# Padding four small tiles so that the buffers behind them in SBUF begin at multiples of 256 bytes

## The chip, the cores and the metric

One Trainium2 chip, of which the kernel uses one core. A core has a tensor engine (PE; its weight loads stand apart as PEld), a vector engine (DVE), a scalar engine (ACT), GpSimd (POOL), a sync engine (SP) that here does little but issue DMAs, and 16 DMA engines that move data between HBM and SBUF, the on-chip memory of 128 partitions. The metric is the time of one execution on the device in microseconds (us); lower is better. "Start" of an SBUF buffer means its byte offset within each partition.

## The reference

Two stages, both in float32. The first is block-sparse attention over 4 batches, 8 heads, 768 positions and a head size of 64: blocks of 32 positions; a query block sees its neighbours, the first and the last block, and three sampled blocks; the first and last query blocks see everything.

```python
scores = scale * np.matmul(q, k.transpose(0, 1, 3, 2))
scores = np.where(mask, scores, -1000000000.0)
scores = scores - np.max(scores, axis=-1, keepdims=True)
attn = np.exp(scores)
attn = attn / (np.sum(attn, axis=-1, keepdims=True) + 1e-09)
return np.matmul(attn, v).astype(np.float32)
```

The second is a feed-forward layer on the 3072 x 512 result, with a rational function between its two products:

```python
h = x @ w_in
P = a[0] + a[1] * h + a[2] * h2 + a[3] * h3
Q = 1.0 + np.abs(b[0]) * np.abs(h) + np.abs(b[1]) * h2
g = P / (Q + 1e-06)
return (g @ w_out).astype(np.float32)
```

The weights come as float64; the kernel turns them into narrower types itself.

## The kernel before

The kernel writes down some thousands of small operations (class `Op`), each with an engine, a price, what it follows and which buffers it takes, and `issue` lays them out on the engines by those prices before the kernel runs. So the order on each engine is fixed when the program is built, and no byte address enters it: changing where a tile lies doesn't change the order.

Keys: a tile of 128 positions of k is loaded (L580, 256-byte runs, one per head and position) into `tt`, `ab`, `sq` for batch 0 and into `ld` for the later ones, transposed on PE (L555) and copied out (L150), for batch 0 into `kall` and later into `kt`, from where L598 stores it to a scratch tensor `ks` in HBM. For the later batches each pair of query blocks gathers its key blocks from `ks` (L777 to L785) into one of three buffers: two halves of `kall`, which is free by then, or `xkg`, a third buffer of the same size. All three are used for the same work in turn.

Queries: L681 loads 128 positions of q into `ldq` in 256-byte runs; PE transposes them (L555).

Values: L913 to L923 gather value blocks from v straight into one of four buffers `vg`, in 512-byte runs. A single block goes to 16 of the 128 partitions, three neighbours to 48, a whole row of blocks (L913) to all 128. The values' product is L944, the scores are L821, the transposes of the probabilities L898. v is also loaded once to find its scale (L646, into `tt`, `ab`, `sq`, `ld`).

Weights: the raw float64 w_in is loaded (L437) into the memory of `wo_l` and `wo_b`; the raw w_out (L432) into `wl`. DVE, ACT and POOL decode both (L446 to L453, and L150, L154, which are one helper for many copies); the working words are `wi` for w_in and `dw` for w_out.

The feed-forward layer runs in units of 256 tokens by 256 hidden columns: products into `ph` (L1040 to L1042), the rational function on ACT and DVE (L1047 to L1085), and products into `acc` (L1097 to L1103). L162 is a filler matmul that the planner puts into PE's gaps in the first part.

SBUF tiles are placed one behind the other, pool by pool, in the order in which a pool first meets them. Three places make small ones: `scales` takes a tile of 4 floats under the names `scw` and `sc1` (three buffers each), `wscale` holds 8 floats, and `most`, in `weights`, takes `sums`, of 8 floats (two buffers). The large buffers behind them begin where these end.

Of the kernel before, what the change touches and what calls it, by code (L numbers as in the profile page):

```python
# [11 lines left out]
F32 = mybir.dt.float32  # L12
# [12 lines left out]
def kernel(  # L25
# [30 lines left out]
    P = 128  # L56
# [10 lines left out]
    NU = NF // 2  # L67
# [8 lines left out]
    const = ctx.enter_context(tc.tile_pool(name="const", bufs=1))  # L76
# [3 lines left out]
    p4 = ctx.enter_context(tc.tile_pool(name="p4", bufs=4))  # L80
    early_cm = tc.tile_pool(name="early", bufs=2)
    early = early_cm.__enter__()
# [50 lines left out]
    def row(eng, steps, after, prio, takes=(), uses=()):  # L133

        o, after = None, list(after)
        for n, (price, run) in enumerate(steps):
            o = Op(eng, price, run, [o] if n else after, prio, takes=() if n else takes, uses=list(uses) + (list(takes) if n else []))
        return o
# [3 lines left out]
    def among(key, home, **prices):  # L142

        d = {{"ve": VE, "sc": SC, "po": PO}[n]: p for n, p in prices.items()}
        return {home: d[home], **(d if key in ALT else {})}

    def times(eng, out, in_, by):

        if eng is nc.scalar:
            nc.scalar.activation(out=out, in_=in_, func=AF.Copy, scale=by)  # L150
        elif eng is nc.vector and isinstance(by, float) and by == 1.0:
            nc.vector.tensor_copy(out=out, in_=in_)
        else:
            eng.tensor_scalar(out=out, in0=in_, scalar1=by, scalar2=0.0, op0=ALU.mult, op1=ALU.add)  # L154
# [181 lines left out]
    def scales(get, name, after, prio, slot=(), finish=None, keep=None):  # L336


        res, d = [], {}
        s_ps = Slot(r_sp)  # L340

        def most():
            d["pt"] = banks[s_ps.buf]
            nc.tensor.transpose(d["pt"][:, :P], get().broadcast_to([P, P]), ident)

        def largest():
            m = p4.tile([P, 4], F32, name=name, bufs=3)
            res.append(m)
            nc.vector.tensor_reduce(out=m[:, 0:1], in_=d["pt"][:, :P], axis=AX.X, op=ALU.max)

        def floor():
            nc.vector.tensor_scalar(out=res[0][:, 0:1], in0=res[0][:, 0:1], scalar1=2.0 ** -100, scalar2=None, op0=ALU.max)

        def exponent():
            mi = res[0].bitcast(I32)
            nc.vector.tensor_scalar(out=mi[:, 1:2], in0=mi[:, 0:1], scalar1=0x7F800000, scalar2=None, op0=ALU.bitwise_and)

        def power():
            m, mi = res[0], res[0].bitcast(I32)
            nc.vector.tensor_scalar(out=mi[:, 2:3], in0=mi[:, 1:2], scalar1=-1.0, scalar2=float((2 * 127 + 14) << 23), op0=ALU.mult, op1=ALU.add)  # L360
            nc.vector.tensor_scalar(out=mi[:, 3:4], in0=mi[:, 1:2], scalar1=float(14 << 23), scalar2=None, op0=ALU.subtract)
            res[:] = [m[:, 2:3], m[:, 3:4]]
            if keep:
                keep(*res)

        def final():
            finish(*res)

        a = Op(TE, 109, most, after, prio, takes=[s_ps])
        a = Op(VE, 260, largest, [a], prio, takes=slot, uses=[s_ps])  # L370
        return row(VE, [(69, floor), (69, exponent), (138, power)] + ([(138, final)] if finish else []), [a], prio, uses=slot), res

    scrap = const.tile([P, 512], F16, name="scrap")

    def head(c, g):

        return 2 * c + g
# [3 lines left out]
    def bound(src, mx):  # L381

        nc.scalar.activation(out=scrap[:, :src.free_size()], in_=src, func=AF.Abs, accum_out=mx)
# [6 lines left out]
    wo_h = const.tile([P, NF, DM], F32R, name="wo_h")  # L390
    wo_l = const.tile([P, NF, DM], BF16, name="wo_l")
    wo_b = const.tile([P, NF, DM], BF16, name="wo_b")
    wscale = const.tile([P, NU], F32, name="wscale")
    in_ready, out_ready, scale_ready, decoded, freed, whole = {}, {}, {}, [], {}, {}


# [5 lines left out]
    def weights():  # L402
# [10 lines left out]
        sums, before, begun = {}, [None, None], {}  # L413

        def raw(u, x):
            x0 = (x // 2 if u == 0 else 2 + x // 2) * NCC
            home = [wo_l, wo_b][x % 2][:, x0:x0 + NCC]
            return home.rearrange("p a n -> p (a n)").bitcast(I32)

        def homes(x):  # L420
            x //= NCC
            return [freed[0 if x < 2 else NG - 1, 2 * (x % 2) + y] for y in range(2)]

        def one(prio, kind, u, x, before):
            d = {}
            s_wl = Slot(r_wl) if kind else None
            s_w = Slot(r_dw) if kind else None

            def load():
                d["ld"] = early.tile([P, 2 * WC], I32, name="wl", bufs=2) if kind else raw(u, x)  # L430
                if kind:
                    nc.sync.dma_start(out=d["ld"], in_=wo64[x * P:(x + 1) * P])  # L432
                    return
                r0 = head(x, 0) * D
                if u == 0 and x == 0:
                    nc.gpsimd.tensor_copy(out=d["ld"][:, 0:1].bitcast(F32), in_=kall[:, 12, 0, 0:1])
                (nc.sync if u > 1 else nc.gpsimd).dma_start(out=d["ld"], in_=wi64[r0:r0 + P, u * 2 * WC:(u + 1) * 2 * WC])  # L437

            def convert(eng):
                d["w"] = early.tile([P, WC], I32, name="dw", bufs=3) if kind else wi[:, x, u].rearrange("p a n -> p (a n)").bitcast(I32)  # L440
                d["words"] = d["ld"].rearrange("p (n w) -> p n w", w=2)
                times(eng, d["w"].bitcast(F32), d["words"][:, :, 1].bitcast(F32), 2.0 ** -112)

            def pack1():
                w = d["w"]
                nc.vector.tensor_scalar(out=w, in0=w, scalar1=3, scalar2=None, op0=ALU.logical_shift_left)  # L446

            def pack2():
                nc.vector.scalar_tensor_tensor(out=d["w"], in0=d["words"][:, :, 0], scalar=29, in1=d["w"], op0=ALU.logical_shift_right, op1=ALU.bitwise_or)  # L449

            def pack3():
                to = d["w"] if kind else d["words"][:, :, 0]
                nc.vector.scalar_tensor_tensor(out=to, in0=d["words"][:, :, 1], scalar=-2 ** 31, in1=d["w"], op0=ALU.bitwise_and, op1=ALU.bitwise_or)  # L453
                if not kind:
                    whole[u, x] = to.bitcast(F32)

            def most():
                if u not in sums:
                    sums[u] = early.tile([P, 8], F32, name="sums")
                bound(whole[u, x], sums[u][:, x:x + 1])  # L460

            def out_high(eng):
                times(eng, wo_h[:, x], d["w"].bitcast(F32), 1.0)

            def out_short(eng):
                times(eng, wo_b[:, x], d["w"].bitcast(F32), 1.0)

            def out_low(eng):
                eng.tensor_tensor(out=wo_l[:, x], in0=d["w"].bitcast(F32), in1=wo_h[:, x].bitcast(F32), op=ALU.subtract)

            wl = [s_wl] if kind else []
            if kind or u > 1:
                o0 = Op(SY, [(475, 524288)], load, [o_setup] if kind else [freed[u - 1, x]], prio - 2, takes=wl, behind=before[kind])
            else:
                o0 = Op(PO, [(700, 524288)], load, [k_evac[0][3]] if u == 0 else [begun[0, x]], -17.0 + 1.2 * x if u else -84, behind=before[kind])
            before[kind] = o0
            w = [s_w] if kind else []
            o = Op(among("c", SC, sc=520, po=588, ve=335), 0, convert, [o0], prio, takes=w, uses=wl)
            if not kind:
                begun[u, x] = o  # L480
            o = Op(VE, 335, pack1, [o], prio, uses=w)
            o = Op(VE, 602, pack2, [o], prio, uses=wl + w)
            o = Op(VE, 602, pack3, [o], prio, uses=wl + w)
            if kind:
                o1 = Op(among("o", SC, sc=520, po=588, ve=335), 0, out_high, [o], prio, uses=w)
                o2 = Op(among("p", PO, po=1225, ve=602), 0, out_low, [o1] + homes(x), prio, uses=w)
                o3 = Op(among("q", SC, sc=520, po=588, ve=335), 0, out_short, [o] + homes(x), prio, uses=w)
                out_ready[x] = [o2, o3]
                decoded.append(o3)
                decoded.append(o2)  # L490
                return o2
            return Op(SC, 613, most, [o], prio)

        group = []
# [755 lines left out]
```

## Time and profile before

| what | value |
|---|---|
| runs | 833.17 us median of 3 (833.16 to 833.39) |
| profiled execution | 832.03 us, of which the span of the core is 830.0 us |
| PE | 782.9 us busy, 94% of the span |
| DVE | 669.0 us, 81% |
| ACT | 571.4 us, 69% |
| POOL | 77.8 us, 9% |
| granted TensorE clock | 0.979 of full speed, mean |
| DMA | 121.27 MB in 224414 packets, 146 GB/s over the span |

The span runs from the first to the last instruction of the core; the 2 us between it and the profiled execution's own time lie around it. A share of busy time is an average over stages that have different limits, so the stages are looked at one by one. The chain of waits is followed back from the last instruction: what stands in it took part in setting the end, and what doesn't had slack. A DMA "issue" is the instruction that starts it, and its time to landing is counted from there.

### The profile page before, as it was taken

The page shows a single profiled execution, that of the slowest core. Times are in us where ns is not written, and L with a number is a line of the kernel's source. Part 1 is how long each engine was busy: PE and PEld are TensorE (multiplying, and loading weights), DVE is VectorE, ACT ScalarE, POOL GpSimd, SP SyncE. Part 2 cuts the span into 40 slices and gives each one's busy share as a digit, 9 for nine tenths or more (in the row PEclk, how much of TensorE's full clock was granted, in tenths as well). Part 3 has the DMA queues.
Part 4 walks back from the last instruction along what each step waited for, and adds up shares of the span by engine and source line. Part 5 has one row for each costly group of instructions (what it writes and reads, how often), then busy time and mean ns, then how long its engine had stood idle before and what let it go on. Part 6 is the DMA issues. An engine that isn't in the chain of part 4 may idle for free.

```text
span 830.0 us, 27500 instructions
## 1 busy us (share of the span) xinstructions
PE 782.9 (94%) x10947; PEld 560.1 (67%) x10947; DVE 669.0 (81%) x1569; ACT 571.4 (69%) x1263; POOL 77.8 (9%) x128
## 2 busy tenths in 40 slices
PE   7787968698999999999999999999999999999997
PEld 3555655476777767677777777677777767767774
DVE  2577999999988985788888884887888886888886
ACT  2386676976776768767576759676676758766563
POOL 2325343233100000000000000000000000000000
PEclk9899997899999999999999999999999999999999
DMA  9988879356675957646746857736667447320000
GB/s 194 207 209 239 206 202 276 93 141 171 143 156 160 216 148 186 170 122 167 152 117 161 191 150 170 195 83 165 143 157 152 116 114 183 69 56 11 1 26 25
DMA packets 224414, 121.27 MB, mean 146 GB/s; under 512 B 62624, under 2 KB 214048, under 8 KB 224288
## 3 DMA queue, kind: packets, MB, share of 16 engines
q1 hardware_dynamic: 223136, 115.34, 57.3%
q0 software_dynamic: 1152, 4.19, 1.8%
q8 instruction: 86, 1.41, 0.8%
q14 instruction: 40, 0.33, 0.1%
HBM read 108.47 MB, written 11.01 MB: 144 GB/s over the span
## 4 chain that ended last, share of the span: by engine, by line
PE 75%; DVE 13%; SPq 4%; ACT 3%; DMA 3%; issue 3%; ACTq 0%
PE acc L1097 10%; PE acc L1103 9%; PE acc L1099 9%; PE ph L1040 9%; PE ph L1042 9%; PE ph L1041 9%; PE m L821 6%; PE av L944 5%; PE m L898 5%; PE acc L162 2%; PE m L555 2%; DMA vg<-in_v_dram 2%; DMA ldq<-in_q_dram 1%; DVE pr L833 1%; DVE dw L449 1%
## 5 line engine op out<-in xcount | busy, mean ns | idle before, releaser
L1040 PE MATMUL ph<-xh,wi 128*128 128x256 f16 x768 | 210.2, 274 | 9.0 <-DVE tt L1057 9.0
L1042 PE MATMUL ph<-xh,wi 128*128 128x256 f16 x768 | 209.9, 273 | 0.0
L1041 PE MATMUL ph<-xl,wi 128*128 128x256 f16 x768 | 209.9, 273 | 0.0
L1047 ACT ACTIVATE sq<-ph,fc 128x512 f32<-128x512 f32 x96 | 66.0, 687 | 112.6 <-PE ph L1042 112.6
L852 ACT ACTIVATE pr<-pr,st 128x256 f32<-128x256 f32 x224 | 110.8, 501 | 14.8 <-DVE st L864 14.8
L1097 PE MATMUL acc<-wo_h,gh 128*128 128x512 f32 x384 | 115.5, 423 | 1.4 <-ACT ld L150 0.7
L1064 DVE SCALAR_TENSOR_TENSOR ab<-sq,absb,ab 128x512 f32<-128x512 f32 x96 | 73.5, 765 | 37.2 <-ACT ab L1061 37.0
L1103 PE MATMUL acc<-wo_b,gl 128*128 128x512 bf16 x384 | 99.4, 382 | 2.1 <-DVE gl L1085 2.1
L1099 PE MATMUL acc<-wo_l,gh 128*128 128x512 bf16 x384 | 100.4, 384 | 0.0
L1040 PEld LDWEIGHTS <-wi 128*128 128x128 f16 x768 | 75.8, 99 | 24.9 <-DVE tt L1057 6.3
L1075 DVE SCALAR_TENSOR_TENSOR gh<-tt,par,rr 128x512 fp32r<-128x512 f32 x96 | 72.9, 760 | 21.0 <-ACT rr L1071 12.3
L150 ACT ACTIVATE pT<-m 128x512 f32<-128x512 f32 x112 | 64.1, 595 | 35.2 <-PE m L898 33.8
L1041 PEld LDWEIGHTS <-wi 128*128 128x128 f16 x768 | 75.4, 98 | 15.5 <-issue 4.0
L833 DVE CUSTOM_DVE_ANT_1 pr<-m,bias 128x256 f32<-128x256 f32 x204 | 76.3, 418 | 11.8 <-PE m L821 11.6
L1042 PEld LDWEIGHTS <-wi 128*128 128x128 f16 x768 | 75.4, 98 | 8.9
L898 PE MATMUL m<-ident,pr 128*128 128x128 f32 x448 | 71.1, 290 | 6.3 <-ACT pT L150 5.7
L1097 PEld LDWEIGHTS acc<-wo_h,gh 128*128 128x128 f32 x384 | 66.7, 192 | 15.2 <-issue 1.2
L1051 ACT ACTIVATE tt<-ph,par,fc 128x512 f32<-128x512 f32 x96 | 74.9, 780 | 0.1
L1054 DVE TENSOR_TENSOR tt<-tt,sq 128x512 f32<-128x512 f32 x96 | 66.7, 694 | 9.4 <-ACT tt L1051 9.4
L898 PEld LDWEIGHTS m<-ident,pr 128*128 128x128 f32 x448 | 63.7, 206 | 15.4 <-ACT pT L150 6.8
L1061 ACT ACTIVATE ab<-ph,fc 128x512 f32<-128x512 f32 x96 | 65.6, 683 | 11.2 <-DVE tt L1081 10.7
L1081 DVE SCALAR_TENSOR_TENSOR tt<-tt,par,ab 128x512 f32<-128x512 f32 x96 | 72.8, 759 | 0.5
(136 smaller groups left out, 1210.0 us busy)
## 6 DMA issues: line engine op xcount, KB each, us to landing
vg<-in_v_dram SPq DMA_DIRECT2D x312, 64.0 KB, 3.8
vg<-in_v_dram SPq DMA_DIRECT2D x88, 192.0 KB, 4.3
kall<-ks SPq DMA_DIRECT2D x138, 64.0 KB, 2.0
wl<-in_moe_w_out_dram SPq DMA_DIRECT2D x16, 512.0 KB, 4.5
vg<-in_v_dram SPq DMA_DIRECT2D x12, 512.0 KB, 4.4
kall<-ks SPq DMA_DIRECT2D x23, 256.0 KB, 3.4
ldq<-in_q_dram SPq DMA_DIRECT2D x20, 256.0 KB, 4.0
out_dram<-ld SPq DMA_DIRECT2D x20, 256.0 KB, 2.8
```

Source lines behind the costliest of these rows:

```text
L833: nc.vector.tensor_tensor_reduce(out=prs[x][:, e, g].rearrange("p (s r) -> p s r", r=BLK), in0=h["sp"][g][:, e], in1=add.rearrange("p (s o ...
L852: nc.scalar.activation(out=prs[x][:, e, g], in_=prs[x][:, e, g], func=AF.Exp, scale=SCALE, bias=st[:, 12 + y:13 + y], accum_out=st[:, 16 + ...
L898: nc.tensor.transpose(pp[:, jj * P:(jj + 1) * P], pr[:, e, g, kt:NS * BLK:2], ident)
L1040: nc.tensor.matmul(o, wh, xh[:, :, cc], start=(cc == 0), stop=False)
L1041: nc.tensor.matmul(o, wh, xl[:, :, cc], start=False, stop=False)
L1042: nc.tensor.matmul(o, wl, xh[:, :, cc], start=False, stop=(cc == NCC - 1))
L1051: nc.scalar.activation(out=d["tt"], in_=d["ph"], func=AF.Identity, scale=d["cst"][:, 3:4], bias=par[:, 2:3])
L1064: nc.vector.scalar_tensor_tensor(out=d["ab"], in0=d["sq"], scalar=absb[:, 1:2], in1=d["ab"], op0=ALU.mult, op1=ALU.add)
L1075: nc.vector.scalar_tensor_tensor(out=d["gh"], in0=d["tt"], scalar=par[:, 0:1], in1=d["rr"], op0=ALU.add, op1=ALU.mult)
L1097: nc.tensor.matmul(acc, g, wo_h[:, f], start=(new and e == 0), stop=False)
L1099: nc.tensor.matmul(acc, g, wo_l[:, f], start=False, stop=False)
L1103: nc.tensor.matmul(acc, g, wo_b[:, f], start=False, stop=(last and e == 1))
```

## The change

Three tiles get wider, and nothing uses the added columns; of `wscale` the first 8 columns are taken.

```diff
-            m = p4.tile([P, 4], F32, name=name, bufs=3)
+            m = p4.tile([P, 12], F32, name=name, bufs=3)
...
-    wscale = const.tile([P, NU], F32, name="wscale")
+    wscale = const.tile([P, 64], F32, name="wscale")[:, 0:NU]
...
-                    sums[u] = early.tile([P, 8], F32, name="sums")
+                    sums[u] = early.tile([P, 32], F32, name="sums")
```

Every engine has the same instructions in the same order as before. What moves is where the tiles behind the padded ones begin. The starts, in the built program:

```
buffer                                    before     rest mod 256   after      rest mod 256
kall, wi, wo_h, wo_l, wo_b                4096 ...   0              the same   0
vg (four)                                 114720 ... 32             114944 ... 0
xh, xl (three each)                       131104 ... 32             131328 ... 0
ldq                                       143392     32             143616     0
kt (first)                                145440     32             145664     0
rr, tt, ab, sq, qt, pT, xn, pr            149536 ... 32             149760 ... 0
ld (three), gh, gl                        192800 ... 32             193024 ... 0
kx and, in its place later, xkg           206176     96             206592     0
ld (four more), kt (second), of later     212320 ... 96             212736 ... 0
wl (two)                                  212384 ... 160            212992 ... 0
dw (three)                                220576 ... 160            221184 ... 0
```

So the buffers of the keys' gather come in two kinds before the change, two in `kall` at a multiple of 256 and `xkg` 96 bytes past one, and in one kind after it. The last byte used moves up by 608.

## Rows read from the trace of the kernel before

**Rows 1.** The page: busy shares, and the chain that ended last by engine

```profile
PE 782.9 (94%) x10947; PEld 560.1 (67%) x10947; DVE 669.0 (81%) x1569; ACT 571.4 (69%) x1263; POOL 77.8 (9%) x128
...
PE 75%; DVE 13%; SPq 4%; ACT 3%; DMA 3%; issue 3%; ACTq 0%
```

**Rows 2.** Four stages: length, busy us of each engine, clock, DMA share, GB/s

```profile
core 0: us, PE busy (x) PEld busy (x) DVE busy (x) ACT busy (x) POOL busy (x), PEclk, DMA share, GB/s
0.00:93.00 93.00, 75.47 (x1422) 48.78 (x1422) 56.63 (x201) 51.37 (x131) 35.14 (x85) 0.93 0.93 213
93.00:230.00 137.00, 115.18 (x1707) 83.20 (x1691) 134.42 (x287) 104.82 (x236) 42.66 (x43) 0.93 0.68 173
230.00:757.00 527.00, 524.00 (x7367) 381.58 (x7370) 419.65 (x995) 376.21 (x838) 0.00 (x0) 1.00 0.60 145
757.00:830.00 73.00, 68.31 (x484) 46.59 (x472) 58.30 (x89) 39.02 (x62) 0.00 (x0) 1.00 0.04 15
```

**Rows 3.** Chain in order of time (start, us, what): its longest DMA-bound pieces

```profile
3.24 1.79 SPq L580
...
8.38 5.92 DMA ldq<-in_q_dram
...
48.28 1.79 SPq L646
...
50.76 0.43 SPq L646
...
52.32 5.70 DMA vg<-in_v_dram
...
68.38 4.35 DMA ldq<-in_q_dram
...
90.32 2.92 DMA vg<-in_v_dram
...
322.15 4.32 DMA vg<-in_v_dram
```

**Rows 4.** DMA issues, whole span: count, KB each, median us to landing

```profile
vg<-in_v_dram SPq DMA_DIRECT2D x312, 64.0 KB, 3.8
...
kall<-ks SPq DMA_DIRECT2D x138, 64.0 KB, 2.0
...
kall<-ks SPq DMA_DIRECT2D x23, 256.0 KB, 3.4
...
xkg<-ks SPq DMA_DIRECT2D x60, 64.0 KB, 2.0
...
xkg<-ks SPq DMA_DIRECT2D x10, 256.0 KB, 3.6
```

**Rows 5.** DMA view, SP's queue (packets, MB, share): xkg alone, 647.1 to 650.4 us

```profile
q1 hardware_dynamic: 1040, 0.52, 56.5%
```

**Rows 6.** The same, kall alone, 671.8 to 673.9 us

```profile
q1 hardware_dynamic: 800, 0.39, 63.7%
```

**Rows 7.** The same, eight gathers into vg alone, 728.7 to 735.5 us

```profile
q1 hardware_dynamic: 1664, 0.79, 53.7%
```

**Rows 8.** The same, one load of vg over 128 partitions, 667.5 to 670.1 us

```profile
q1 hardware_dynamic: 1040, 0.52, 70.5%
```

**Rows 9.** L449 and L821 by tile, L821 from 250 us on: min/median/max ns

```profile
L449 DVE SCALAR_TENSOR_TENSOR dw<-wl,dw x16: 653/680/1725, 67.2 to 214.0; 128x512 int32<-128x512 int32 x16
L449 DVE SCALAR_TENSOR_TENSOR wi<-wo_l,wi x8: 678/691/1076, 24.7 to 145.0; 128x512 int32<-128x512 int32 x8
...
L821 PE MATMUL m<-kall,qt x1152: 216/344/400, 266.9 to 745.5; 64*32 64x256 f32 x85, 64*32 64x192 f32 x55, 64*32 64x64 f32 x52
...
L821 PE MATMUL m<-xkg,qt x576: 216/344/400, 253.6 to 717.0; 64*32 64x256 f32 x85, 64*32 64x192 f32 x54, 64*32 64x64 f32 x53
```

**Rows 10.** Three stretches around one fall of the clock, columns as in rows 2

```profile
35.24:83.03 47.79, 40.46 (x972) 28.40 (x970) 35.72 (x119) 36.82 (x96) 18.42 (x40) 1.00 0.83 218
83.03:86.44 3.41, 3.41 (x31) 1.75 (x32) 2.48 (x7) 0.60 (x2) 1.38 (x3) 0.50 1.04 214
86.44:120.50 34.06, 28.11 (x486) 20.52 (x470) 33.25 (x69) 25.42 (x66) 14.10 (x13) 1.00 0.84 214
```

**Rows 11.** The chain again, the idle stretch on PE ahead of that fall

```profile
80.01 2.54 issue
```

## The prediction

> **What bounds the kernel now.** I read the page first: PE is busy for 94% of the span, and the chain that ended last lies on PE for 75%, on DVE for 13%, and on DMAs and SP's issuing together for 7% [rows 1]. Such shares mix stages, so the table by stage comes next [rows 2]. From 230 to 757 us PE is busy 524.00 of 527.00 us at the full clock: PE alone sets the time there, and a DMA that lands earlier finds its cover unchanged. From 93 to 230 us DVE is busy 134.42 of 137 us: DVE sets it. The last 73 us move 15 GB/s: no DMA matters but the final store. What is left for a change of DMA writes is the first 93 us, where the DMA share is 0.93 at 213 GB/s and no engine is full (PE 75.47 of 93 us, DVE 56.63). The chain in order of time shows what counts there [rows 3]: four waits for a landing in the first 93 us (5.92 and 4.35 us for queries, 5.70 and 2.92 us for values), and one later on, 4.32 us at 322 us. They sum to 23.21 us, 10.27 for queries and 12.94 for values. Beside them SP is held up when it issues: two issues on the chain take 1.79 us where their like takes 0.43, that is 2 x 1.36 = 2.7 us which I count as pressure from DMAs that are still under way. So some 26 us of 830 hang on how fast DMAs write to the buffers that move. The rest of SP's 4% is issuing, which no address changes.
>
> **The change part by part.** It removes and adds no instruction and moves none on any engine or queue. The widened columns are never written or read, so widening itself costs nothing. Only starts differ, and this costs or saves time only where the duration of a transfer or of an instruction depends on its start. The trace of before has a built-in comparison for that, since the kernel puts the same work on buffers of both kinds.
>
> *Engines.* The score matmuls read their keys from `kall` (start at a multiple of 256) or `xkg` (96 past one): 216/344/400 ns as least, median and most, for both, over 1152 and 576 instructions [rows 9]. DVE's decoding step reads and writes `dw` and `wl` (160 past) with a median of 680 ns, `wi` and `wo_l` (at a multiple) with 691 ns [rows 9]. The second pair is 11 ns, 1.6%, the other way, but the two kinds run in different parts of a busy stage and their ranges overlap, so I take the exact pair on PE and cost engine work at 0. As an upper bound, 1.6% of DVE's 134.42 us in the stage that it bounds is +2.2 us.
>
> *DMA writes.* The gathers of keys go to all three buffers in turn. In 64 KB pieces the median to landing is 2.0 us into `kall` (138 loads) and 2.0 us into `xkg` (60 loads) [rows 4]. In 256 KB pieces it is 3.4 against 3.6 us (23 and 10 loads), 5.6% in favour of the multiple of 256. Packet times say the same: SP's queue alone, share x 16 engines x window / packets. Into `xkg`, 0.565 x 16 x 3300 / 1040 = 28.7 ns [rows 5]; into `kall`, 0.637 x 16 x 2100 / 800 = 26.8 ns [rows 6], 6.6% less, in part because the second window has a larger share of the small closing packets (32 of 800 against 16 of 1040). So aligning a write is worth between 0 and 6.6% of its time. On the 26 us that is 0 to 1.7 us. I take the 64 KB pair, which has the most loads and the size of the values' pieces: no difference within its rounding, 0.05 of 2.0 us or 2.5%, which would be 0.65 us; half of that is 0.3 us, and this I take.
>
> *DMA reads from SBUF.* The stores of keys (L598) and of the output begin at multiples of 256 too. Nothing on the chain waits for the former; the latter counts only with the last store. By the same 0 to 6.6%, on a transfer of some 2 us, this is below 0.15 us. I take 0.
>
> *Raw output weights.* `wl` feeds POOL, ACT and DVE between 60 and 215 us; no wait for its landing is among the long pieces of the chain. 0.
>
> Sum: 832.03 - 0.3 = 831.7 us for an execution like the profiled one. The median of the runs is 1.14 us above that execution, so 833.17 - 0.3 gives **832.9 us**. The measurement of this kernel can tell some 0.2%, 1.7 us, from no change, so I call this the same.
>
> **The rivals.** *First: every misaligned write pays the full price of the upper rows.* Then 6.6% of 26 us goes, 1.7 us, and the time is 831.5 us, just at the bound of what is measurable. For it: both the 256 KB loads and the packet times lean this way [rows 4 to 6]. Against it: the 198 loads of 64 KB show nothing. The Trainium skill speaks for this rival: its page "DMA: Bandwidth & Descriptors", under "How a descriptor splits into AXI transactions", says that a run which does not start at a multiple of 256 bytes begins with a transaction from the boundary below and pays beats for bytes it doesn't use; by its count a 256-byte run starting at 32 would cost 9 beats instead of 8 and a 512-byte run 17 instead of 16. By that, as an estimate, the waits would shrink by 10.27 / 9 + 12.94 / 17 = 1.9 us, to 831.3 us. The trace agrees with it in the sign and, for the larger loads, in the size, but not for the 64 KB pair. Chance 0.13.
>
> *Second, clearly faster: the values' gathers are slow because of their start.* They take 3.8 us for 64 KB where the keys' take 2.0 [rows 4], and eight of them alone show 0.537 x 16 x 6800 / 1664 = 35.1 ns a packet [rows 7], against 28.2 ns (0.705 x 16 x 2600 / 1040) for the load of the same buffers over 128 partitions [rows 8]. Most writes of a gather go to 16 partitions, so they may crowd one path into SBUF, where a run cut into more pieces would cost more than in an open one. If alignment took away that whole excess, 20% of 12.94 us is 2.6 us, with 6.6% of the queries' 10.27 us another 0.7: 833.2 - 3.3 = 829.9 us. If it brought the landing down to the keys' 2.0 us, three waits would lose 1.8 us each, 5.4 in all, and the time would be 827.1 us. Against it: the load over 128 partitions has the same rest of 32 and is not slow, so it is the narrow target that crowds, which the change leaves as it is. Chance 0.17, most of it at the nearer end.
>
> *Third, slower: one more stretch at the half clock.* Where PE idles in the early part, the granted clock has fallen to half: after 2.54 us of idle at 80 us [rows 11] the stretch from 83.03 to 86.44 us ran at 0.50, between stretches at 1.00 [rows 10]. The fillers on PE stand at fixed places, so when loads land a little earlier, PE comes earlier to a wait for DVE, ACT or POOL and idles there longer. If one more such stretch falls to 0.50, PE does half its work in 3.41 us and loses up to 1.7 us: 834.9 us. It decides only if PE has no slack in it; where DVE sets the pace the loss is covered. For it: the clock of the first 230 us is 0.93 already, so it is near its edge [rows 2]. Against it: shifts of 0.3 us are small beside these stretches, and a stretch may be won as well as lost. Chance 0.13; DVE's 2.2 us from above is no more than a tail of the same sign, 0.02.
>
> **How the numbers follow.** The forecast, no change beyond 0.6 us either way, has the remaining 0.55. Faster by more than 0.2% is the second rival (0.17), somewhat over half of the first (0.07) and a little of the forecast's tail (0.03): 0.27. Slower by more than 0.2% is the third rival with DVE's tail, 0.15, less what stays below 1.7 us, 0.02: 0.13. That leaves 0.60. The range takes in the forecast, the first rival, the nearer end of the second and the third: 829.8 to 834.9 us.
>
> **What would show it.** Right: after the change the 64 KB gathers into `kall` and `xkg` still have equal medians near 2.0 us, those into `vg` stay near 3.8 us, the first wait for queries is still close to 5.9 us, matmuls and DVE steps keep their durations to the nanosecond or two, and the four stages keep their lengths within 0.5 us. Wrong on the fast side: the 64 KB median for `vg` falls by more than 0.2 us and the four early waits shrink together, so that the stage that ends at 93 us ends some 2 us earlier. Wrong on the slow side: a stretch at 0.50 that wasn't there before 230 us, or DVE's 512-column steps some 10 ns longer throughout.

## The result, and the profile after

The change is faster: 823.81 us, median of 4 runs (823.72 to 823.95), against 833.28 us (833.16 to 833.48) for the kernel before beside it. The ratio is 0.9893 (95% interval 0.9879 to 0.9907), 9.5 us or 1.1%. The forecast was no change, 832.9 us, a gain of 0.3 us, in a range of 829.8 to 834.9 us; the gain is some thirty times that.

The page of the kernel after, its busy shares and its chain by engine [rows 1 of before]:

```profile
PE 779.4 (95%) x10947; PEld 558.8 (68%) x10947; DVE 670.1 (82%) x1569; ACT 570.7 (69%) x1263; POOL 76.2 (9%) x128
...
PE 78%; DVE 13%; ACT 3%; DMA 2%; issue 2%; SPq 1%; ACTq 0%
```

Every engine has as many instructions as before; PE is 3.5 us less busy, DVE 1.1 us more. The chain has less of SP, from 4% of 830 us to 1% of 822, and less of the DMAs and of "issue". The same stages as in [rows 2]:

```profile
0.00:93.00 93.00, 79.87 (x1553) 51.83 (x1554) 66.28 (x226) 58.51 (x144) 35.59 (x86) 1.00 0.86 228
93.00:230.00 137.00, 115.46 (x1668) 84.35 (x1667) 133.45 (x276) 102.30 (x230) 40.63 (x43) 0.93 0.63 174
230.00:757.00 527.00, 523.87 (x7343) 381.89 (x7342) 418.93 (x992) 375.93 (x836) 0.00 (x0) 1.00 0.52 143
```

The first 93 us now hold 1553 matmuls instead of 1422 and 226 DVE instructions instead of 201, while the DMAs are busy for less of the time (0.86 for 0.93) and move more (228 for 213 GB/s). From 230 to 757 us nothing changes but the DMA share. The two profiled executions took 832.03 and 823.95 us, so their traces have 8.1 of the 9.5 us to show; the rest is the distance of each from the median of its runs. The chain in order of time shows where they come from [rows 3]:

```profile
3.24 1.82 SPq L580
...
7.81 5.00 DMA ldq<-in_q_dram
...
46.96 5.56 DMA sq<-in_v_dram
52.54 3.98 DMA vg<-in_v_dram
...
71.17 1.29 PE m L821 x80
...
84.09 0.69 DVE wo_l L453
...
314.27 4.28 DMA vg<-in_v_dram
```

The pieces at 71.17 and 84.09 us have these counterparts in the kernel before:

```profile
77.06 1.29 PE m L821 x81
...
93.24 0.68 DVE wo_l L453
```

The first queries land at 12.81 us (7.81 + 5.00) instead of 14.30. The score matmuls that began at 77.06 us begin at 71.17, the DVE step of 93.24 us at 84.09. So 1.5 us are won by 13 us, 5.9 by 77 and 9.1 by 93. The values' wait that began at 322.15 us begins at 314.27: 7.9 us remain there, so 1.3 us were given back in between, in the stage that DVE sets, and the rest is carried to the end, where the spans differ by 8.1 us. Of the five waits in [rows 3], those at 68.38 and 90.32 us are gone from the chain, and the one at 52 us, 5.70 us before, is 3.98 us. A wait of 5.56 us for `sq` stands ahead of it that the chain before doesn't have; there SP's issuing filled that time. The DMA view of the whole run [rows 4]:

```profile
vg<-in_v_dram SPq DMA_DIRECT2D x312, 64.0 KB, 2.7
...
kall<-ks SPq DMA_DIRECT2D x138, 64.0 KB, 2.0
...
vg<-in_v_dram SPq DMA_DIRECT2D x12, 512.0 KB, 4.5
...
xkg<-ks SPq DMA_DIRECT2D x60, 64.0 KB, 2.0
```

This is the heart of it. The 64 KB pair on which the forecast stood is unchanged: 2.0 us into `kall` and into `xkg`. So is the load of `vg` over all 128 partitions (4.4 us before, 4.5 after). But the 312 narrow gathers into `vg`, the same buffers, land in 2.7 instead of 3.8 us. For the eight gathers that stand alone near the end, now at 720.6 to 727.4 us, SP's queue shows [rows 7]:

```profile
q1 hardware_dynamic: 1653, 0.78, 40.0%
```

That is 0.400 x 16 x 6800 / 1653 = 26.3 ns a packet instead of 35.1. Their landings moved less: the six of 64 KB from 3.5 to 3.2 us in the median, the two of 192 KB from 4.0 to 4.8. Then a view that the prediction doesn't use, SP's queue from 8.4 to 10 us, where the first key and query tiles come in 256-byte runs over 128 partitions. Before:

```profile
DMA packets 1380, 0.35 MB, mean 217 GB/s; under 512 B 1380, under 2 KB 1380, under 8 KB 1380
...
q1 hardware_dynamic: 1380, 0.35, 134.7%
```

After:

```profile
DMA packets 1822, 0.46 MB, mean 288 GB/s; under 512 B 1822, under 2 KB 1822, under 8 KB 1822
...
q1 hardware_dynamic: 1822, 0.46, 127.3%
```

The share is over 100% in both: packets of one engine overlap there, so their durations are no measure of the rate. The rate was 217 GB/s before and is 288 now. That something behind the engines sets it is my reading; no row shows what.

### The profile page after: what moved, and what is told of

Read it like the earlier page. It is cut to its first block, busy times and chain, and to the rows that moved or that the text cites. A ratio compares the mean times of both kernels' runs of the same rounds, so it can differ in the third digit from the quotient of the medians.

```text
span 821.9 us, 27500 instructions
## 1 busy us (share of the span) xinstructions
PE 779.4 (95%) x10947; PEld 558.8 (68%) x10947; DVE 670.1 (82%) x1569; ACT 570.7 (69%) x1263; POOL 76.2 (9%) x128
## 3 DMA queue, kind: packets, MB, share of 16 engines
q1 hardware_dynamic: 223136, 115.34, 51.2%
## 4 chain that ended last, share of the span: by engine, by line
PE 78%; DVE 13%; ACT 3%; DMA 2%; issue 2%; SPq 1%; ACTq 0%
PE acc L1097 10%; PE ph L1040 9%; PE acc L1103 9%; PE acc L1099 9%; PE ph L1041 9%; PE ph L1042 9%; PE m L821 6%; PE av L944 6%; PE m L898 5%; PE acc L162 2%; PE m L555 2%; DVE pr L833 1%; PE m L982 1%; DVE dw L449 1%; DMA vg<-in_v_dram 1%
## 5 line engine op out<-in xcount | busy, mean ns | idle before, releaser
L898 PE MATMUL m<-ident,pr 128*128 128x128 f32 x448 | 69.4, 286 | 4.7 <-ACT pT L150 4.0
L1057 DVE SCALAR_TENSOR_TENSOR tt<-ph,fc,tt 128x512 f32<-128x512 f32 x96 | 71.5, 744 | 0.7
```

The costliest lines, as they stand in the source:

```text
L898: nc.tensor.transpose(pp[:, jj * P:(jj + 1) * P], pr[:, e, g, kt:NS * BLK:2], ident)
```

## The experiments

My theory after the result: a run that does not start at a multiple of 256 bytes in SBUF is written in one more piece, and this costs only where writes are dense, as in the narrow gathers and in the 256-byte runs of the first tiles. The runs below test at which starts and in which transfers it costs; the pieces are in no view, since SP's queue shows 223136 packets before and after. Rivals: that the size that counts is 64 bytes, or 512; that the distance from the boundary is paid; that one kind of load makes the whole gain; that any shift of the layout moves this kernel by chance. The kernels ran in three groups, each on one chip beside the kernel before; there the runs of one kernel scatter by some us (the kernel before: 826.4 to 835.9 us), so ratios with intervals are given, and the transfer views carry most of the verdicts. Expected times of the first group were written for a kernel before of 833.28 us; it took 831.71 there, so they are read as distances from it.

**The change again.** Twice, as a yardstick for each of the later groups; no edit.

> The changed kernel itself, on the chip of this group of runs and beside runs of the kernel before there, since the runs of the first group scatter more than those shown with the case. If its gain belongs to the layout: a ratio of 0.986 to 0.992, 64 KB into vg in 2.7 to 2.9 us. If much of it belonged to one chip: a ratio of 0.994 or more.

> The changed kernel beside its two halves and beside the kernel before, on one chip, so that the parts can be added up: a ratio of 0.987 to 0.992.

Measured: 822.69 us, ratio 0.9894 (0.9838 to 0.9950); and 825.30 us, 0.9918 (0.9896 to 0.9941). The gain belongs to the layout, not to one chip. The narrow gathers took 2.9 us in both.

**The two halves.** For `vg` alone:

```diff
-    wscale = const.tile([P, NU], F32, name="wscale")
+    wscale = const.tile([P, 64], F32, name="wscale")[:, 0:NU]
...
     vgs = [const.tile([P, H, 2 * D], F32, name=f"vg{i}") for i in range(4)]
+    gap = const.tile([P, 8], F32, name="gap")
```

and for all but `vg`:

```diff
-            m = p4.tile([P, 4], F32, name=name, bufs=3)
+            m = p4.tile([P, 12], F32, name=name, bufs=3)
...
-                    sums[u] = early.tile([P, 8], F32, name="sums")
+                    sums[u] = early.tile([P, 32], F32, name="sums")
...
     vgs = [const.tile([P, H, 2 * D], F32, name=f"vg{i}") for i in range(4)]
+    gap = const.tile([P, 56], F32, name="gap")
```

> Only the four vg buffers begin at a multiple of 256; every other tile keeps its rest of before (32, 96 or 160), by a gap of 32 bytes behind vg. Theory A (the narrow gathers into vg crowd SBUF and are what the change relieves): most of the 9.5 us is kept, 825 to 827 us; 64 KB gathers into vg land in a median of 2.7 to 3.0 us as after the change, the first wait for queries stays at 5.9 us. Theory B (every misaligned run costs, and the first loads of keys and queries count most): under half of the gain, 829 to 832 us. Theory C (the clock of the first 93 us brings it, whatever moves a load): no clear split between this run and its counterpart, their gains don't add up to 9.5 us.

> The counterpart: vg keeps its rest of 32, everything else begins where the change puts it, at a rest of 0. Theory A: 830 to 832 us; the wait for the first queries falls from 5.9 to 5.0 us and PE starts 1.5 us earlier, but 64 KB gathers into vg still land in a median of 3.6 to 3.8 us. Theory B: 824 to 828 us. Theory C: a gain that doesn't complement the one of vg alone to 9.5 us.

> vg alone aligned, again, beside the whole change. If the two halves add up (each buffer's transfers save on their own): this half and the other together give the whole, about 0.994 and 0.996. If they hang together (SP's queue and PE's waits in the first 93 us are held by whichever load is still slow): the halves together give clearly less than the whole, 0.995 to 0.997 and 0.997 to 0.999 against 0.989.

> All but vg aligned, again. Additive: 0.995 to 0.997. Hanging together: 0.997 to 0.999, with the first 1.5 us of PE's earlier start visible in the trace but most of it lost by 93 us.

Measured, `vg` alone: 828.12 us, 0.9955 (0.9931 to 0.9978), and 827.55 us, 0.9946 (0.9924 to 0.9967). All but `vg`: 829.19 us, 0.9983 (0.9960 to 1.0005), and 828.76 us, 0.9963 (0.9945 to 0.9981). Both fall between the forecasts of theory A and theory B, so neither holds alone. In the first group the halves sum to 0.62%, short of the 1.07% of the result, as theory C has it, but the whole change did not run beside them there. In the last group, where it gave 0.82%, the halves give 0.54 and 0.37%: they add up within their intervals. The times alone are weak evidence, since a layout further down with every moved start at a rest of 128 also came out 0.46% faster. The transfers separate cleanly. The first run with `vg` alone, gathers over the whole span and SP's queue from 8.4 to 10 us:

```profile
vg<-in_v_dram SPq DMA_DIRECT2D x312, 64.0 KB, 2.9
...
DMA packets 1357, 0.34 MB, mean 213 GB/s; under 512 B 1357, under 2 KB 1357, under 8 KB 1357
```

The first run with all but `vg`:

```profile
vg<-in_v_dram SPq DMA_DIRECT2D x312, 64.0 KB, 3.8
...
DMA packets 1800, 0.46 MB, mean 285 GB/s; under 512 B 1800, under 2 KB 1800, under 8 KB 1800
```

Each buffer's own start decides its own transfers: 2.9 us but 213 GB/s in the one, 3.8 us but 285 GB/s in the other. The second runs showed 3.0 us and 218 GB/s, and 3.7 us and 229 GB/s; in the last the share was only 100.8%, so the queue was less full in that stretch. The waits follow. The first one for queries in the second run of each half, `vg` alone and then all but `vg`:

```profile
8.42 5.76 DMA ldq<-in_q_dram
```

```profile
8.64 4.67 DMA ldq<-in_q_dram
```

**The start, step by step.** The pads of the other two tiles as in the change, and `wscale` of another width each time: 8 floats leave the buffers behind it at a rest of 32, 16 at 64, 32 at 128, 56 at 224, and 128 at a multiple of 512. One of the edits, against the changed kernel, the others alike:

```diff
-    wscale = const.tile([P, 64], F32, name="wscale")[:, 0:NU]
+    wscale = const.tile([P, 16], F32, name="wscale")[:, 0:NU]
```

> A control: the two other pads are made, the one of wscale is not, so nearly every moved buffer stays at a rest of 32 (the key, weight and late load buffers go from 96 and 160 to 32). Boundary theory: no change, a ratio of 0.997 to 1.003, 64 KB into vg 3.7 to 3.9 us, first key loads 215 to 220 GB/s. If any shift of a layout can move the time of this kernel by chance, a ratio outside of that with transfer times as before.

> The change's own layout with all the moved buffers at a rest of 64 mod 256 in place of 0. Boundary theory (a run that starts off a multiple of 256 is cut in one more piece, wherever it starts): about as slow as before, 831 to 835 us; 64 KB into vg 3.6 to 3.9 us; the first key loads move 210 to 225 GB/s. Line theory (only starts off a multiple of 64 cost, by a partly written line): as fast as after the change, 823 to 825 us, 2.7 us, 285 GB/s. Beats theory (what lies between the boundary below and the start is paid): somewhat slower than before, 834 to 838 us.

> The same at a rest of 128. Boundary theory: 831 to 835 us, as at 64 and 32. Line theory: 823 to 825 us. Beats theory: slower the farther the start is from the boundary below, 836 to 845 us.

> All moved buffers at a rest of 224. Boundary theory: first key loads 215 to 220 GB/s, 64 KB into vg 3.5 to 3.9 us, time within 0.5% of before. Beats theory: the slowest of all, key loads under 200 GB/s, vg over 4 us.

> The change with wscale 256 bytes wider still: all moved buffers at a multiple of 512 (the change leaves them at 256 past one). If 256 is the size that counts: as after the change, a ratio within 0.2% of its, vg 2.7 to 2.9 us, key loads 285 GB/s. If 512 counted too, for the 512-byte runs of the gathers: vg under 2.6 us and another 1 us or more off the time.

| start | ratio to before (95% interval) | first tiles, 8.4 to 10 us | 64 KB into vg |
|---|---|---|---|
| 32 past a multiple of 256 | 0.9972 (0.9945 to 1.0000) | 217 GB/s | 3.9 us |
| 64 past | 0.9991 (0.9972 to 1.0010) | 214 GB/s | 3.6 us |
| 128 past | 0.9954 (0.9928 to 0.9981) | 218 GB/s | 3.5 us |
| 224 past | 0.9985 (0.9957 to 1.0014) | 218 GB/s | 3.8 us |
| multiple of 512 | 0.9896 (0.9844 to 0.9949) | 251 GB/s | 2.9 us |
| the change, in the last two groups | 0.9894, 0.9918 | 284, 280 GB/s | 2.9 us |

At 64 past the boundary SP's queue from 8.4 to 10 us reads

```profile
DMA packets 1361, 0.34 MB, mean 214 GB/s; under 512 B 1361, under 2 KB 1361, under 8 KB 1361
```

So 64 is not enough, 512 brings no more than 256, and for the first tiles it doesn't matter how far from the boundary a run starts: 214 to 218 GB/s for every rest other than 0. The gathers took 3.5 to 3.9 us at these rests, in no order of the distance. The line theory and the beats theory fall; what the boundary theory forecast for the transfers came out. (At 512 the share in that stretch was 110.9% instead of 127.3%, so the queue was less full there; the gathers and the time are those of the change.) What stays unexplained is the ratio at 128, 0.5% under 1 with unimproved first tiles and gathers only slightly better; the control at 32, with hardly anything moved in its rest, also lies 0.3% under 1. That any shift of the layout moves the time by so much is not excluded. The gain of the whole change, 0.8 to 1.1% each time, is about twice that; the times of the two halves are not.

**One pad of the three.**

```diff
-    wscale = const.tile([P, NU], F32, name="wscale")
+    wscale = const.tile([P, 64], F32, name="wscale")[:, 0:NU]
```

> The pad of wscale alone: vg, the first key, value and query tiles at a rest of 0; wl at 128, the third key buffer and the late load tiles at 64. If the first 93 us make the whole gain, in which wl and the late tiles hold nothing up: as the whole change, within 0.2% of its ratio. If the raw output weights or the late tiles count: a third or more of the gain is missing.

Measured: 825.10 us, 0.9920 (0.9900 to 0.9940), against 0.9918 for the whole change on the same chip. The first tiles came at 277 GB/s, the narrow gathers in 2.8 us. The other two pads, which align the raw output weights, the third key buffer and the late load tiles, bring nothing that these runs show. No version beat the change.

## Why the prediction was wrong, point by point

**What bounds the kernel.** Right for the stages: the gain is made before 93 us, where DMAs are dense and no engine is full, and 230 to 757 us did not move. Wrong on SP: I had counted 2.7 us of it as pressure from transfers, in two issues that take 1.79 us each on the chain. The one of L580 at 3.24 us still takes 1.82 us, and one of L646, at 43.92 us, takes 1.57 us: the first was no such pressure, and the second hardly changed. SP went from 4% to 1% of the chain, some 33 to some 8 us, but that doesn't measure the gain either: the page shows 2% for SP with all starts at 64 and at 224, which were as slow as before. That SP had been late rather than slow, its issuing hidden behind PE once the loads come earlier, would fit the traces of before and after; no run tests it.

**Engine work at 0.** Right. In the kernel after, L821 from 250 us on still takes 216/344/400 ns, and DVE's step on `dw`, now at a multiple of 256, still 680 ns, on `wi`, which did not move, still 691 [rows 9]:

```profile
L449 DVE SCALAR_TENSOR_TENSOR dw<-wl,dw x16: 653/680/1732, 62.9 to 206.0; 128x512 int32<-128x512 int32 x16
L449 DVE SCALAR_TENSOR_TENSOR wi<-wo_l,wi x8: 677/691/1074, 23.2 to 137.4; 128x512 int32<-128x512 int32 x8
...
L821 PE MATMUL m<-kall,qt x1152: 216/344/400, 258.9 to 737.4; 64*32 64x256 f32 x85, 64*32 64x192 f32 x55, 64*32 64x64 f32 x52
```

So the 11 ns between the two kinds in DVE's step was where and when they ran, and the upper bound of 2.2 us on the slow side was empty.

**DMA writes: the step that failed.** The whole change gave 0.8 to 1.1%, 7 to 9.5 us, where this term had 0.3 us, from "the 64 KB pair, which has the most loads and the size of the values' pieces". The pair was a fair comparison of two starts, and its equal 2.0 us was true before and after. But it compares them where writes have room: 512-byte runs spread over 128 partitions, few at a time. The values' gathers have the same size and go to 16 partitions, and the first tiles come in runs of 256 bytes, all engines at once. There the start was worth 29% of the landing (3.8 to 2.7 us; 24% with the 2.9 us of the repeats) and a third of the rate (217 to 288 GB/s), not the 0 to 6.6% of my bounds. I took a price where writes have room and applied it where they are dense. The trace of before held the clue: 217 GB/s with a share of 134.7%, that is packets that overlap in a full queue.

**The raw output weights and stores.** 0 was right for the weights, by the run with one pad. The stores were not tried by themselves.

**The first rival** (every write pays the full price, 831.5 us) had the wrong form: crowded writes pay far more, the others nothing. The Trainium skill's page "DMA: Bandwidth & Descriptors", section "How a descriptor splits into AXI transactions", says that a transfer is split at multiples of 256 bytes, and the trace fits that, with the gain at a rest of 0 alone. By the beats that the same section of the Trainium skill counts from the boundary below, as an estimate, a 256-byte run would cost 9 beats at a rest of 32 but 15 at 224; the trace disagrees for these writes, 217 and 218 GB/s. The prediction's remark that the larger loads agree with that count in size is a misreading: it set their 5.6% beside the count for a start 32 past the boundary, but `xkg` starts 96 past it, where the same count gives 19 beats for 16, as an estimate.

**The second rival** had the right place and direction for one half, with a chance of 0.17: the values' gathers are slow because of their start. My argument against it was that the load over 128 partitions has the same rest and is not slow, so the narrow target crowds, which the change leaves as it is. Both halves of that are true and don't contradict: it takes the narrow target and the start together. Its price for the gathers, 2.6 to 5.4 us, fits what `vg` alone gave, 0.45 and 0.54% or 3.7 to 4.5 us of 830. Too low was its price for the rest, 0.7 us for the queries: all but `vg` gave 0.17 and 0.37%, 1.4 to 3.1 us, though the first of these can't be told from nothing. It had not thought of the first tiles as a full queue.

**The third rival** went the other way. In the profiled executions the clock's mean in the first 93 us rose from 0.93 to 1.00 [rows 2, 10]: the idle of 2.54 us ahead of the fall at 83 us [rows 11] has a counterpart of

```profile
74.12 0.35 issue
```

and the stretch from 35.24 to 83.03 us, at the full clock in both [rows 10], now holds 44.16 us of PE and 40.63 us of DVE for 40.46 and 35.72:

```profile
35.24:83.03 47.79, 44.16 (x981) 31.37 (x977) 40.63 (x131) 38.17 (x98) 21.42 (x39) 1.00 0.81 225
```

So more work gets done at an equal clock, too. Two other traces say the same: the control at 32 and the repeated change, 835.73 and 822.27 us, have the same clock in the first 93 us, 0.96, and differ in the work done by then, 200 against 222 DVE instructions (the control first):

```profile
0.00:93.00 93.00, 75.06 (x1364) 48.42 (x1368) 55.35 (x200) 49.91 (x128) 34.05 (x85) 0.96 0.94 211
```

```profile
0.00:93.00 93.00, 82.93 (x1549) 53.82 (x1550) 65.79 (x222) 57.81 (x142) 36.54 (x86) 0.96 0.86 230
```

But the clock has a part in the times. In the second group the kernel before took 826.38 us in an execution at a mean granted clock of 0.989, and 833.81 in one at 0.976. The change mostly ran at a higher clock, 0.982 to 0.990. Compared at one clock, in the last group, it took 825.31 us at 0.982, where the kernel before took 832.75 and 833.07; 827.09 at 0.983, against 829.63 and 832.07; and 825.30 at 0.985, against 829.25 and 831.58. So most of the gain is there at an equal clock, some 5.5 us in the mean of these three against 6.8 us between the medians, and a part may come from fewer stretches at half the clock. Whether these follow from the earlier loads no run tests.

## What to carry to other kernels

Where DMAs write densely to SBUF in runs of 256 or 512 bytes, as in this kernel's first 93 us, let the buffers start at multiples of 256 bytes; one small tile ahead of the big ones is enough to spoil it for all. Take the price of a transfer's property from rows where transfers are as dense as where it matters: equal times where there is room say nothing about a full queue, and a DMA share above 100% says that packet durations are not the rate. Don't read a gain off an engine's share of the chain: SP's fell to 2% in layouts that gained nothing.

## What the hardware showed that I had not expected

Writes of 256-byte runs over 128 partitions ran at 213 to 218 GB/s from any start that was not a multiple of 256, whether 32, 64, 128 or 224 past it, and at 277 to 288 GB/s from a multiple, where the queue's share was 122.5% or more (251 and 229 GB/s at shares of 110.9 and 100.8%). Loads of 512 KB in 512-byte runs over 128 partitions did not change (4.4 and 4.5 us).

PE's idle stretches that the profile calls "issue" are shorter with the change. The longest before and its counterpart after, on the chain:

```profile
25.56 4.47 issue
```

```profile
24.07 1.98 issue
```

The two repeats of the change had 3.07 and 2.95 us here, the control at 32 had 3.65. They lie inside one group of score matmuls, and the profile shows no releaser. But their ends follow the queue named "instruction", which the DMA view counts on the same 16 engines. Before, one of its packets, of 16 KB, was under way from 27.53 to 28.60 us, and PE went on at 30.03; after, one was under way from 23.16 to 24.56 us, and PE went on at 26.05. In all the 14 traces of this case the chain of the first 95 us has 30 idle stretches of this kind of over 1 us, and each ends 1.3 to 1.9 us after the end of such a packet. That PE waits there for its own program is thus likely, though no run here changes these packets; why they come earlier when the data loads do stays open.
